# Which ring of SBUF buffers holds the early products of the first layer: four buffers of `stg` in place of two of `p`

## The chip, the cores and the metric

The kernel runs on one core of one Trainium2 chip. The metric is the device time of one execution in microseconds (us); lower is better. The kernel before was timed three times.

## The reference, cut to what matters

```python
# 1. a recurrence over 768 tokens, for 4 batches and 8 heads of width 48
for t in range(S):
    cur = np.einsum('bhd,bhe->bhde', u[None] * kt, vt)
    y[:, :, t] = np.einsum('bhd,bhde->bhe', rt, state + cur)
    state = w[None, :, :, None] * state + np.einsum('bhd,bhe->bhde', kt, vt)
# 2. x: the 3072 tokens of y, 384 wide
a = x @ w1            # 384 x 1024
b = x @ w2            # 384 x 1024
x2 = (a * b @ w3) @ w_out
# 3. second layer
h = x2 @ w_in         # 384 x 2048
out = (h * np.cos(h)) @ w_out2
```

The weights come as 64-bit floats and are decoded on the chip.

## The kernel before, in words

**Stages.** The recurrence is computed in 12 chunks of 64 tokens (`att_scores`, `att_mask`, `att_y`, `att_x`, `att_state`; `prep_*` scale the inputs). Tiles carry the chunk's number: `sc3_1` are the scores of chunk 3, half 1; `y3_1` and `st3_1` its output and state sums; `xp3_0` its transposes (L569). `att_x` copies these to `xh` (L574) and `xl` (L575), the high and low parts of the activations that the first layer multiplies. Two chunks fill one of six blocks `j` of 512 tokens.

**First layer.** For each block `j` and each of eight column tiles `m`, `ab(j, m)` computes two sums `a` and `b` in PSUM, each by three times three matmuls (high times high, high times low, low times high: L273, L274, L275). ScalarE then copies `a` to a buffer `p` in SBUF (L772), VectorE multiplies `b` into it (L773), and GpSimd issues a store of the product to DRAM, `pd` (L774). The copy and the product are issued with priority. `p0_4` is the product of `j` = 0, `m` = 4. The first two products of block 0 are computed in two halves of 256 tokens.

**Fold.** `w3 @ w_out` is multiplied once into `w34` (`fold_load`, `fold_mm`). Later the products are read back, multiplied by `w34` (`p3`), and the second layer follows (`stage_a` to `p4`).

**Rings of buffers.** `kt_(tag, ...)` gives the next of a fixed number of buffers: `p` has two, `stg` four. A buffer is given out again once its last reader is done; for a product that reader is its store. `stg` is used for a constant of the warm-up matmuls, later for half of the fold's decoded weights, for `x2` and for the output. PSUM has eight banks: three for `a` and `b`, two for the recurrence, three for sums.

**Order.** Each engine executes its instructions in the order of its queue. A scheduler fixes that order when the program is built, from its own estimate of when operands and buffers are ready. So a buffer that comes free earlier can move instructions. The program's order around the first layer is written out: `ORDER` lists the products, `SLOTS` says how many steps of the recurrence go ahead of each, `FOLD` how many of the fold. The fold's first step stands ahead of entry 14.

**Loads.** SP issues all loads. The scores need `rd` and `kd`, whose single buffers are loaded again for the next chunk when the scores of this one are done (L367), and then scaled on VectorE (L486).

Of the kernel before, what the change touches and what calls it, by code (L numbers as in the profile page):

```python
# [184 lines left out]
def kernel(  # L185
# [19 lines left out]
    with ExitStack() as own:  # L205
        held = own.enter_context(tc.tile_pool(name="held", bufs=1))
        dram = own.enter_context(tc.tile_pool(name="slow", bufs=1, space=DRAM))
        flag = held.tile([1, 1], I32, name="flag")
        chunked(
            tc, flag, rd_in, kd_in, rt_in, kt_in, vt_in, wT_in, u_in, w1_in, w2_in, w3T_in, wo_in, wi2_in, wo2_in, out  # L210
        )
        odd = nc.values_load(flag[0:1, 0:1], min_val=0, max_val=48)
        with tc.If(odd > 0):
            xc = dram.tile([out.shape[0], 384, 512], F32, name="xc")
            sequential(tc, rt_in, kt_in, vt_in, w_in, u_in, xc)
            plain(tc, xc, w1_in, w2_in, w3T_in, wo_in, wi2_in, wo2_in, out)
# [3 lines left out]
def chunked(  # L220
# [41 lines left out]
    def kt_(tag, shape, nm, dt=F32):  # L262
        return keep.tile(list(shape), dt, tag=tag, name=nm, bufs=BUFS[tag])

    def bank(nm, tag):
        return psum.tile([128, 512], F32, tag=tag, name=nm, bufs={"ab": 3, "att": 2, "acc": 3}[tag])
# [5 lines left out]
    def mm3(o, wh, wl, xh, xl, first, last):  # L272
        nc.tensor.matmul(o, wh, xh, start=first, stop=False)  # L273
        nc.tensor.matmul(o, wh, xl, start=False, stop=False)  # L274
        nc.tensor.matmul(o, wl, xh, start=False, stop=last)  # L275
# [7 lines left out]
    def flush():  # L283
        while late:
            late.pop(0)()
# [311 lines left out]
    halves, whole = [slice(0, 256), slice(256, 512)], slice(0, 512)  # L597
# [41 lines left out]
    def w12(m, n):  # L639
        g, i = divmod(m, 4)  # L640
        fs = slice(i * 128, (i + n) * 128)
        for which, hi, lo in ((1, w1h, w1l), (2, w2h, w2l)):
            if g not in hi:
                hi[g] = wp.tile([128, 3, 512], F32R, tag=f"g{g}", bufs=4, name=f"w{which}h{g}")
                lo[g] = wp.tile([128, 3, 512], F32R, tag=f"g{g}", bufs=4, name=f"w{which}l{g}")
            decode(w12_id[which, m], (hi[g][:, :, fs], lo[g][:, :, fs]))
# [6 lines left out]
    for ps in range(3):  # L653
        n = 128 * min(3, NM1 - 3 * ps)
# [42 lines left out]
    def fold_step(n):  # L697
        for _ in range(n):
            if folds:
                it = folds.pop(0)  # L700
                fold_load(*it)
                fold_pend.append(it)
            if len(fold_pend) > (2 if folds else 0):
                if not folds:
                    flush()
                fold_mm(*fold_pend.pop(0))
# [48 lines left out]
                nc.scalar.copy(s, acc[j][e])  # L755
                nc.sync.dma_start(out=x2d[j][:, e, :], in_=s)

    def ab(j, m, cols=slice(0, 512)):
        g, i = divmod(m, 4)
        fs = slice(i * 128, (i + 1) * 128)  # L760
        n = cols.stop - cols.start
        a = bank(f"a{j}_{m}", "ab")[:, 0:n]
        b = bank(f"b{j}_{m}", "ab")[:, 0:n]
        for t, wh, wl in ((a, w1h, w1l), (b, w2h, w2l)):
            for kk in range(3):
                mm3(
                    t, wh[g][:, kk, fs], wl[g][:, kk, fs], xh[j][:, kk, cols], xl[j][:, kk, cols], kk == 0, kk == 2
                )
        p = kt_("p", (128, 512), f"p{j}_{m}")[:, 0:n]

        with tc.high_priority(offset=-80):
            nc.scalar.copy(p, a)  # L772
            nc.vector.tensor_tensor(out=p, in0=p, in1=b, op=ALU.mult)  # L773
        nc.gpsimd.dma_start(out=pd[j][m][:, cols], in_=p)  # L774
# [43 lines left out]
    decays()  # L818
    flush()
    ab(0, 0, halves[0])  # L820
    prep_u(1)
    prep_g(1)
# [7 lines left out]
    att_state(1, 0)  # L830
    flush()
    ab(0, 1, halves[0])
    att_x(1, 1)
    att_state(1, 1)
# [11 lines left out]
    def advance(n):  # L846
        for _ in range(n):
            att_slot(*next(slots, (NSTEP, 0)))

    for i, (j, m) in enumerate(ORDER):  # L850
        advance(SLOTS[i])
        if i in (1, 6):
            w12({1: 4, 6: 6}[i], 2)
        fold_step(FOLD[i])
        flush()
        ab(j, m, halves[1] if j == 0 and m < 2 else whole)
    while folds or fold_pend:
        fold_step(1)
    att_cm.__exit__(None, None, None)
# [16 lines left out]
    for i in range(NBLK * NM1):  # L876
        j, m = divmod(i, NM1)
# [64 lines left out]
    for it in items + [None] * 5:  # L942
        if it:
            j, m = it
# [80 lines left out]
```

## Time and profile before

| what | value |
|---|---|
| time, median of 3 runs | 863.75 us (861.83 to 864.93) |
| the profiled execution | 865.14 us, of which 863.4 us from the first to the last instruction (the span) |
| mean granted TensorE clock | 0.99 of full speed |
| busy share of the span | PE 97%, VectorE (DVE) 64%, ScalarE (ACT) 48%, GpSimd (POOL) 4% |
| stores of products | 46 whole ones of 256 KB, median 2.8 us to landing |

PE is TensorE. In the profile, a bracket behind an instruction gives the time that its engine stood idle ahead of it and what ended that. The chain is the sequence of work that ended last, followed back from the end.

### The profile page before, as it was taken

To read this page: it belongs to the slowest core of one execution; us is meant where nothing else is said; L and a number is where in the kernel's file an instruction comes from. 1 tells how busy PE (TensorE), PEld (TensorE's weight loads), DVE (VectorE), ACT (ScalarE), POOL (GpSimd) and SP (SyncE) were. 2 spreads that over 40 slices of the span, in tenths; PEclk is the share of its full clock that TensorE was granted. 3 is DMA by queue.
4 is the path that set the end of the run, shared out by engine and by line. 5 is a ranking of instruction groups with operands and counts; after the bars stand their busy time and mean duration, and the time that the engine had idled before them with its cause. 6 is when DMAs were issued, how large, how long until landed. Compare 5 with 4: busy or idle time off the path is not lost.

```text
span 863.4 us, 14166 instructions
## 1 busy us (share of the span) xinstructions
PE 840.5 (97%) x5630; PEld 682.9 (79%) x5634; DVE 554.8 (64%) x839; ACT 415.6 (48%) x708; POOL 35.9 (4%) x66
## 2 busy tenths in 40 slices
PE   6987999999999999999999999999999999999997
PEld 3775778888888888888888888888888888888885
DVE  8876977786555534498956655655655655655552
ACT  4764555544553531255446445445545544544442
POOL 3000010010100001000000000000000000000000
PEclk9988999999999999999999999999999999999998
DMA  8757566565343263288952002001001100100101
GB/s 254 208 182 221 163 199 210 177 206 151 113 149 110 71 209 132 90 305 296 326 177 74 1 1 73 1 1 59 15 1 38 36 0 15 59 0 1 38 1 40
DMA packets 41161, 95.04 MB, mean 110 GB/s; under 512 B 4736, under 2 KB 6400, under 8 KB 41088
## 3 DMA queue, kind: packets, MB, share of 16 engines
q1 hardware_dynamic: 37072, 81.28, 30.0%
q0 software_dynamic: 3872, 12.59, 3.9%
q8 instruction: 46, 0.75, 0.4%
q10 hardware_dynamic: 144, 0.20, 0.1%
q14 instruction: 27, 0.22, 0.1%
HBM read 72.03 MB, written 22.02 MB: 109 GB/s over the span
## 4 chain that ended last, share of the span: by engine, by line
PE 94%; DVE 2%; DMA 1%; ACT 1%; issue 1%; ACTq 0%; DVEq 0%
PE p L274 12%; PE p L273 12%; PE p L275 12%; PE h L275 8%; PE h L273 8%; PE h L274 8%; PE a L273 4%; PE b L273 4%; PE b L275 4%; PE b L274 4%; PE a L274 4%; PE a L275 4%; PE y L554 3%; PE sc L518 2%; PE hps L409 2%; PE st L591 2%
## 5 line engine op out<-in xcount | busy, mean ns | idle before, releaser
L921 ACT ACTIVATE u<-h,qbias 128x512 f32<-128x512 f32 x96 | 66.2, 689 | 138.0 <-PE h L275 138.0
L922 DVE TENSOR_SCALAR n<-u 128x512 f32<-128x512 f32 x96 | 41.1, 428 | 138.0 <-ACT u L921 138.0
L275 PE MATMUL h<-x2h,wil 128*128 128x512 f32 x288 | 113.2, 393 | 0.0
L273 PE MATMUL h<-x2h,wih 128*128 128x512 f32 x288 | 113.1, 393 | 0.0
L274 PE MATMUL p<-gl,woh 128*128 128x512 f32 x288 | 113.1, 393 | 0.0
L274 PE MATMUL h<-x2l,wih 128*128 128x512 f32 x288 | 113.0, 392 | 0.0
L275 PE MATMUL p<-gh,wol 128*128 128x512 f32 x288 | 113.0, 392 | 0.0
L273 PE MATMUL p<-gh,woh 128*128 128x512 f32 x288 | 113.0, 392 | 0.0
L924 ACT ACTIVATE u<-n 128x512 f32<-128x512 f32 x96 | 60.9, 634 | 65.1 <-DVE n L923 65.1
L930 DVE TENSOR_TENSOR u<-u,h 128x512 f32<-128x512 f32 x96 | 66.0, 687 | 16.7 <-ACT u L924 16.7
L773 DVE TENSOR_TENSOR p<-p,b 128x512 f32<-128x512 f32 (+1 forms) x50 | 33.1, 661 | 62.4 <-PE b L275 35.7
L923 DVE SCALAR_TENSOR_TENSOR n<-n,u 128x512 f32<-128x512 f32 x96 | 66.4, 692 | 3.3
L936 DVE TENSOR_TENSOR gl<-u,gh 128x512 fp32r<-128x512 f32 x96 | 65.7, 685 | 0.7 <-ACT gh L932 0.7
L274 PEld LDWEIGHTS p<-gl,woh 128*128 128x128 f32 x288 | 54.1, 188 | 12.4
L275 PEld LDWEIGHTS h<-x2h,wil 128*128 128x128 f32 x288 | 54.1, 188 | 12.3
L273 PEld LDWEIGHTS h<-x2h,wih 128*128 128x128 f32 x288 | 54.1, 188 | 12.3
L274 PEld LDWEIGHTS h<-x2l,wih 128*128 128x128 f32 x288 | 54.1, 188 | 12.2
L273 PEld LDWEIGHTS p<-gh,woh 128*128 128x128 f32 x288 | 54.1, 188 | 12.2
L275 PEld LDWEIGHTS p<-gh,wol 128*128 128x128 f32 x288 | 54.1, 188 | 12.2
L772 ACT COPY p<-a 128x512 f32<-128x512 f32 (+1 forms) x50 | 28.3, 568 | 67.3 <-PE a L275 56.0
L273 PE MATMUL a<-xh,w1h 128*128 128x512 f32 (+1 forms) x150 | 60.4, 403 | 0.0
L932 ACT CAST gh<-u 128x512 fp32r<-128x512 f32 x96 | 58.9, 613 | 0.8 <-DVE u L930 0.8
(163 smaller groups left out, 1717.5 us busy)
## 6 DMA issues: line engine op xcount, KB each, us to landing
pr<-pd SPq DMA_DIRECT2D x48, 256.0 KB, 4.1
pd<-p POOLq DMA_DIRECT2D x46, 256.0 KB, 2.8
raw<-in_wo_dram SPq DMA_DIRECT2D x12, 768.0 KB, 5.0
raw<-in_w3T_dram SPq DMA_DIRECT2D x8, 768.0 KB, 5.0
raw<-in_wi_dram SPq DMA_DIRECT2D x8, 768.0 KB, 5.6
raw<-in_w_dram SPq DMA_DIRECT2D x6, 768.0 KB, 5.7
x2d<-x SPq DMA_DIRECT2D x18, 256.0 KB, 5.5
x2s<-x2d SPq DMA_DIRECT2D x18, 256.0 KB, 3.3
```

The source lines that it names most:

```text
L273: nc.tensor.matmul(o, wh, xh, start=first, stop=False)
L274: nc.tensor.matmul(o, wh, xl, start=False, stop=False)
L275: nc.tensor.matmul(o, wl, xh, start=False, stop=last)
L772: nc.scalar.copy(p, a)
L773: nc.vector.tensor_tensor(out=p, in0=p, in1=b, op=ALU.mult)
L921: head[0] = nc.scalar.activation(out=u, in_=h, func=AF.Identity, scale=INV_2PI, bias=qbias).ins
L922: nc.vector.tensor_scalar_add(out=n, in0=u, scalar1=RND)
L923: nc.vector.scalar_tensor_tensor(out=n, in0=n, scalar=RND, in1=u, op0=ALU.subtract, op1=ALU.subtract)
L924: nc.scalar.activation(out=u, in_=n, func=AF.Sin, scale=-TWO_PI)
L930: nc.vector.tensor_tensor(out=u, in0=u, in1=h, op=ALU.mult)
L932: nc.scalar.copy(gh, u)
L936: nc.vector.tensor_tensor(out=gl, in0=u, in1=gh.bitcast(F32), op=ALU.subtract)
```

## The change

A new argument of `ab`, `early`, true unless it is given, takes the product's buffer from the ring `stg` instead of `p`. The loop over `ORDER` gives it as true for entries 0 to 12. The two half products that are computed ahead of the loop are early as well. The remaining 35 entries keep the ring `p`. No instruction is added or removed.

```diff
-    def ab(j, m, cols=slice(0, 512)):
+    def ab(j, m, cols=slice(0, 512), early=True):
...
-        p = kt_("p", (128, 512), f"p{j}_{m}")[:, 0:n]
+        p = kt_("stg" if early else "p", (128, 512), f"p{j}_{m}")[:, 0:n]
...
-        ab(j, m, halves[1] if j == 0 and m < 2 else whole)
+        ab(j, m, halves[1] if j == 0 and m < 2 else whole, early=i < 13)
```

The built programs of before and after differ in the order of the queues and in what some instructions wait for. A number at the end of a name only tells buffers apart; in square brackets stand the semaphores that an instruction waits for, and `DMASW` is that of a store of GpSimd (the stores take `DMASW0` to `DMASW7` in turn).

ScalarE, at the second half of chunk 3's masks (`xa`, `xb`: operands of `y3_0`; `yt3_0`: the copy of `y3_0`):

```order
 L501 COPY zb_137<-kt_130 64x768 [waits Activation_49]
-L539 COPY xa_131<-am_133 64x512 [waits DVE_49,Activation_49]
-L540 COPY xb_132<-am_133 64x512 [waits Activation_49]
-L539 COPY xa_131<-am_133 64x512 [waits DVE_49,Activation_49]
-L540 COPY xb_132<-am_133 64x512 [waits Activation_49]
-L772 COPY p0_4_1076<-a0_4_1056 128x512 [waits DMASW4_49,PE_49]
+L772 COPY p0_4_1076<-a0_4_1056 128x512 [waits DMASW2_49,PE_49]
+L539 COPY xa_131<-am_133 64x512 [waits DVE_49,Activation_49]
+L540 COPY xb_132<-am_133 64x512 [waits Activation_49]
+L539 COPY xa_131<-am_133 64x512 [waits DVE_49,Activation_49]
+L540 COPY xb_132<-am_133 64x512 [waits Activation_49]
 L556 COPY yt3_0_1033<-y3_0_1016 128x384 [waits PE_49,Activation_49]
```

The copy of `a0_4` moves ahead of the masks' copies, and it waits for the third store (a half product) where it waited for the fifth (`p0_2`).

PE, from the last matmuls of `a0_1`'s second half to `y2_0`; before:

```order
L274 MATMUL a0_1_835<-xl0_381,w1h0_361 128x256
L275 MATMUL a0_1_835<-xh0_380,w1l0_362 128x256
L554 MATMUL y2_0_775<-va_134,xa_131 64x48 [waits DMAHW5_49,Activation_49]
L554 MATMUL y2_0_775<-vb_135,xb_132 64x48 [waits DMAHW6_49,Activation_49]
L554 MATMUL y2_0_775<-va_134,xa_131 64x48
```

and after:

```order
L275 MATMUL a0_1_835<-xh0_380,w1l0_362 128x256
L273 MATMUL b0_1_836<-xh0_380,w2h0_370 128x256 [waits Activation_49]
L274 MATMUL b0_1_836<-xl0_381,w2h0_370 128x256
L275 MATMUL b0_1_836<-xh0_380,w2l0_371 128x256
L273 MATMUL b0_1_836<-xh0_380,w2h0_370 128x256
```

The nine matmuls of `b0_1`, which stood behind `y2_0` and `st2_0`, now stand ahead of them. Likewise the last three of `b0_4` and the first six of `a0_5` move ahead of `y3_0`.

PE, between `b0_5` and the next block's products; before:

```order
L274 MATMUL b0_5_1142<-xl0_381,w2h1_824 128x512
L275 MATMUL b0_5_1142<-xh0_380,w2l1_825 128x512
L273 MATMUL a1_0_1181<-xh1_878,w1h0_361 128x512 [waits Activation_49]
L274 MATMUL a1_0_1181<-xl1_879,w1h0_361 128x512 [waits DVE_49]
L275 MATMUL a1_0_1181<-xh1_878,w1l0_362 128x512
```

and after:

```order
L275 MATMUL b0_5_1142<-xh0_380,w2l1_825 128x512
L273 MATMUL a1_0_1181<-xh1_878,w1h0_361 128x512 [waits Activation_49]
L518 MATMUL sc4_0_1229<-rd_127,kd_128 64x64 [waits DMAHW1_49,DMAHW3_49,DVE_49,PE_49]
L521 MATMUL sc4_0_1229<-rd_127,kd_128 64x64 [waits DMAHW4_49,DMAHW2_49]
L518 MATMUL sc4_0_1229<-rd_127,kd_128 64x64
```

The scores of chunk 4 stood behind `a1_0`, `b1_0`, `a1_1` and `b1_1`; now they come after the first matmul of `a1_0`, ahead of the other 35. On VectorE the order changes accordingly, and most of the fold's decoding moves behind later products. GpSimd's order is the same.

## Rows read from the trace of the kernel before

**Rows 1.** The page: busy time of each engine, share of the span, instructions.
```profile
PE 840.5 (97%) x5630; PEld 682.9 (79%) x5634; DVE 554.8 (64%) x839; ACT 415.6 (48%) x708; POOL 35.9 (4%) x66
```

**Rows 2.** Windows by stage: stretch, length, busy of PE, PEld, DVE, ACT, POOL, PEclk, DMA, GB/s.
```profile
40.00:80.00 40.00, 34.81 (x459) 28.56 (x457) 33.63 (x45) 21.55 (x37) 2.70 (x5) 0.91 0.69 203
80.00:120.00 40.00, 36.43 (x317) 29.63 (x318) 32.13 (x41) 18.72 (x32) 4.13 (x7) 0.91 0.59 185
120.00:160.00 40.00, 40.00 (x509) 32.40 (x508) 30.29 (x41) 25.04 (x42) 2.70 (x5) 1.00 0.67 201
```

**Rows 3.** PE's timeline, 50 to 172 us: start, duration, instruction, idle before.
```profile
50.97 0.45 PE L554 MATMUL y<-va,xa 128*64 128x48 f32 x2 [2.84 <-DMA rd<-in_rd_dram]
54.77 0.58 PE L273 MATMUL b<-xh,w2h 128*128 128x256 f32 x1
56.64 0.41 PE L275 MATMUL b<-xh,w2l 128*128 128x256 f32 x1
83.57 0.34 PE L554 MATMUL y<-va,xa 128*64 128x48 f32 x1 [5.34 <-ACT yt L556]
171.71 0.42 PE L273 MATMUL fa<-fwh,w3h 128*128 128x384 f32 x1
```

**Rows 4.** The chain, 73 to 87 us: start, duration, what.
```profile
73.99 8.48 DMA pd<-p
83.03 0.49 ACT yt L556
83.57 1.95 PE y L554 x32
85.52 0.83 PE xp L569 x3
86.35 0.43 PE a L273
```

**Rows 5.** ScalarE's timeline, 76 to 83 us.
```profile
76.36 0.62 ACT L540 COPY xb<-am 64x512 f32<-64x512 f32 x1
82.55 0.58 ACT L772 COPY p<-a 128x512 f32<-128x512 f32 x1 [5.57 <-DMA pd<-p]
```

**Rows 6.** Waits of the whole span: who waited for whom, total, times, longest.
```profile
ACT p L772 <- DMA pd<-p: 11.1, 3, 5.6
```

**Rows 7.** Stores of products, from issue to landing: minimum, median, maximum.
```profile
DMA to landing us min/median/max: 2.3/2.9/8.5
```

**Rows 8.** Windows of one microsecond, columns as in Rows 2.
```profile
50.00:51.00 1.00, 0.03 (x1) 0.03 (x1) 1.00 (x3) 0.67 (x2) 0.00 (x0) 0.55 1.01 209
81.00:82.00 1.00, 0.00 (x0) 0.00 (x0) 0.00 (x0) 0.00 (x0) 0.00 (x0) 0.50 0.99 397
```

**Rows 9.** The chain, 121 to 126 us, at the full clock.
```profile
121.92 1.07 PE y L554 x32
122.99 0.48 PE xp L569 x3
123.47 0.24 PE a L273
124.88 0.85 PE st L591 x32
```

**Rows 10.** VectorE's timeline, 60 to 150 us; the last row is the product `p1_7`.
```profile
60.13 0.56 DVE L575 TENSOR_TENSOR xl<-xp,xh 128x384 fp32r<-128x384 f32 x1 [2.46 <-ACT xh L574]
79.66 1.23 DVE L486 TENSOR_TENSOR rd<-rd,t 128x1024 f32<-128x1024 f32 x1 [1.68 <-DMA rd<-in_rd_dram]
87.38 0.95 DVE L332 TENSOR_TENSOR w1l<-dt,w1h 128x768 fp32r<-128x768 f32 x1
88.24 1.22 DVE L486 TENSOR_TENSOR kd<-kd,t 128x1024 f32<-128x1024 f32 x1
149.72 0.69 DVE L773 TENSOR_TENSOR p<-p,b 128x512 f32<-128x512 f32 x1 [1.63 <-ACT p L772]
```

**Rows 11.** A window from `rd`'s scaling to `p1_2`'s product, columns as in Rows 2.
```profile
79.66:107.44 27.78, 23.87 (x208) 19.44 (x209) 21.02 (x27) 14.22 (x23) 2.17 (x4) 0.88 0.57 179
```

## The prediction

> **What bounds the kernel now.** I read the page's busy times first: TensorE (PE) is busy 97% of the span, the others far less [rows 1]. So time can come only from PE's idle time and from stretches at a lowered clock. The windows by stage say where these are: of 40 us PE works 34.81 in 40 to 80 us and 36.43 in 80 to 120 us, at a mean granted clock of 0.91; from 120 us on it works 40.00 of 40 at 1.00 [rows 2]. Behind 120 us PE is the bound without a gap, so whatever makes it reach that point earlier should last to the end; the other engines must then keep up in a schedule that is shifted earlier.
>
> PE's timeline shows two large gaps: 2.84 us ahead of 50.97 and 5.34 us ahead of 83.57 [rows 3]. The chain of waits explains the second. The store of `p0_2` is issued at 73.99 and lands 8.48 us later, at 82.47; then come `yt` at 83.03, the copy of `y3_0`, and `y3_1` on PE at 83.57 [rows 4]. ScalarE's timeline has the link between them: it is through with the masks' copies at 76.36 + 0.62 = 76.98, and the next thing in its queue is the copy of `a0_4` into a `p` buffer, which waits 5.57 us for that store [rows 5]. The copy of `y3_0` only stands behind it. Over the whole span such waits of the copy come to 11.1 us in three, but only this one stands in the chain [rows 4, 6].
>
> The gap costs more than its length. In the 1-us windows the clock is granted at 0.50, the level of 1.2 GHz, at 81 us, after PE has stood since 78.23 (83.57 − 5.34); it is 0.55 at 50 us, behind the other gap [rows 3, 8]. At that level `y3_1` takes 1.95 us, its transposes 0.83 and each row of `a0_5` 0.43 [rows 4]; the same work at the full clock takes 1.07, 0.48 and 0.24 [rows 9].
>
> **The change, part by part.** Nothing is added or removed, so the sum has only waits, order and clock.
>
> *The wait of `p0_4`.* From the four buffers, its copy waits for the third store, a half product's, where it waited for the fifth. It also stands ahead of the masks' copies now. The third store belongs to the second half of `p0_0`, whose matmuls precede those of `b0_1` at 54.77 [rows 3]; even at the longest landing, 8.5 us [rows 7], it is down before 73.99. The copy's 0.58 us then lies under the 8.48 us in which ScalarE had slack, while PE has the last three matmuls of `b0_4` and six of `a0_5` to do. Behind 76.98 ScalarE goes straight to `yt`, 0.49 [rows 4], so `y3_1` can start at 77.5 in place of 83.57: 6.1 us. Seven matmuls of `a0_5` that followed then are done ahead of it: 7 × 0.24 = 1.7 [rows 9]. Together **7.8**. It is more than the 5.34 of the gap, because it assumes that the matmuls which moved ahead find room; what bounds that comes under "the first gap".
>
> *The clock behind the gap.* PE does not stand, so the clock has no reason here to fall: (1.95 − 1.07) + (0.83 − 0.48) + 3 × (0.43 − 0.24) = **1.8** [rows 4, 9].
>
> *The first gap.* `b0_1`'s nine matmuls move out of 54.77 to 57.05 (56.64 + 0.41) into the wait ahead of 50.97; what they took behind it, 2.28 us at the lowered clock, is gone [rows 3]. In their place five matmuls of `a0_2` come into that slow stretch, 5 × (0.43 − 0.24) = 0.95 longer than they would be later. That leaves some 1.3 us of room for nine more matmuls ahead of `y3_0`, 9 × 0.24 = 2.2: if the clock stays down here, `y3_0` starts up to 0.9 us late, which takes 0.9 from the 7.8. If the clock stays up, since PE stands less, the lost half comes back, and the masks may come earlier too: VectorE stands 2.46 us at 60 us for the transposes that PE brings [rows 10]. I bound this term by −0.9 and +2.5 and take **+0.5**: the clock was still lowered after 2.84 us of standing, and `b0_1` at full clock fills less than half of that.
>
> *The scores of chunk 4, moved forward.* `sc4_0` now stands ahead of 35 matmuls, and PE's queue waits there for `kd`'s scaling on VectorE. PE is there about 77.5 + 1.07 + 0.48 + 0.85 + 12 × 0.24 = 82.8 (`y3_1`, transposes, state sums, the rest of `a0_5`, `b0_5` and one of `a1_0`) [rows 9]. `rd`'s scaling waited for its load until 79.66 [rows 10], and that load needs only the scores of chunk 3, which hardly move. Behind it stand `w1l` (0.95), `xl` (0.56), the first step of a decode (about as `xl`) and `kd` (1.22): by these rows 79.66 + 1.23 + 0.95 + 0.56 + 0.56 + 1.22 = 84.2; starts overlap by some 0.1 each, so about 83.7. PE waits some **−0.8**, with bounds of 0 (the decode elsewhere, PE later) and −1.4.
>
> *What must keep up.* If PE is some 9 us earlier at 107 us, VectorE must be nearly so. From `rd`'s scaling at 79.66, a load's time that does not move, to the product of `p1_2` at 107.44 it works 21.02 of 27.78 us [rows 11]: it can gain 6.8, and the other 2.5 must come from the time between a product and the next use of its PSUM bank, and from the decode that moves behind. I take nothing here, and price it as a rival. The fold's decoding is pushed back on VectorE: its second half now precedes `p1_7`'s product (149.72) and is needed by matmuls at 171.71 [rows 3, 10]; 22 us, less the shift of 9, hide it.
>
> Sum: 7.8 + 1.8 + 0.5 − 0.8 = **9.3 us**. The profiled execution took 865.14, so 855.8; it lay 1.4 above the median of the runs, so **854.4 us** against 863.75.
>
> **The rivals.**
> - *The masks become the bound.* If the scores' masks and the products on VectorE come late between 85 and 120 us, part of the gap opens again there. For it speaks that VectorE's room is 6.8 and the shift 9.3 [rows 11]; against it, that much of its work in the stretch (the decode) is moved behind. Gain 5 to 8: about **857.3**.
> - *The wait is not what it seems.* If another thing held ScalarE, say a store that is quick and a semaphore that comes late for another reason, the masks' copies and `yt` would only trade places: **863.7**. Against it stands the DMA share of 0.99 in the wait with nothing busy [rows 8]. The Trainium skill, "DMA: Bandwidth & Descriptors", section "Anatomy of one DMA — SWDGE (gpsimd) path", gives some 2.0 us plus the bytes at 436 GB/s for such a store; an estimate by it for 256 KB is 2.6 us, the store would land at 76.6, ahead of the masks' end, and the change would win nothing. The median of the stores, 2.9, is close to that, the 8.48 of this one is not [rows 4, 7], and the trace decides.
> - *Slower: PE waits at `sc4_0`.* The 35 matmuls that covered the loads and scalings of `rd` and `kd` now stand behind the wait. Were `kd` scaled as late as before, at 88.24 + 1.22 = 89.46 [rows 10], PE would stand 6.7 us, not 0.8, and lose perhaps 1.5 to a lowered clock: gain 2, **861.9**. It turns into a loss when the scaling ends later than some 91.5. For that the loads would have to land 8 us later than now, in competition with the stores that are issued earlier; the store that took 8.48 shows that this is possible at this DMA share. At 96 us: **868**.
>
> **How the numbers follow.** Forecast 0.70, its own range 852 to 856.5 (the bounds of the first gap and of `sc4_0`: sum 7.3 to 12.1, the upper end hardly reached in full); masks 0.15; no effect 0.07; the third rival 0.08, of which 0.06 for a loss and 0.02 for the small gain. A measurement of this kernel can tell about 0.3%, 2.6 us, from no change: faster 0.85 (the first two), within 0.09, slower 0.06. To leave out no more than 2 in 10, the range runs from 851.5 to 859.0.
>
> **What the profile of after would show.** ScalarE's wait of 5.57 for `pd` and PE's gap ahead of `y3_1` gone; the clock near 1.00 from 75 to 90 us; PE busy some 39 of 40 in 80 to 120 us; the waits of the copy for stores from 11.1 to 1 or less. A PE gap ahead of `sc4_0` names the third rival, gaps of PE behind masks or products in 90 to 120 the first. I am wrong if a gap of more than 2 us opens anywhere behind 75 us, or if stores issued earlier slow the loads of chunks 3 and 4.

## The result, and the profile after

The changed kernel took 855.42 us (median of six runs, 853.77 to 856.81), the kernel before 863.54 us in the six runs timed with it. The ratio is 0.9906 with a 95% interval of 0.989 to 0.9921, that is 6.8 to 9.5 us less; the forecast was 854.4. The profiled execution has a span of 853.5 us and a mean granted clock of 1.00.

The windows by stage, columns as in [rows 2]:

```profile
40.00:80.00 40.00, 38.17 (x545) 31.47 (x544) 38.25 (x51) 27.06 (x47) 3.25 (x6) 1.00 0.76 237
80.00:120.00 40.00, 39.93 (x361) 31.10 (x359) 27.96 (x36) 19.71 (x32) 3.78 (x7) 1.00 0.57 179
120.00:160.00 40.00, 40.00 (x484) 32.68 (x483) 33.97 (x44) 24.34 (x41) 3.25 (x6) 1.00 0.65 193
```

PE stands 1.83 us in 40 to 80 us where it stood 5.19, and 0.07 in 80 to 120 us where it stood 3.57. The clock is at its higher level in all three. All that is left of the gaps, but for 0.09 us, is in PE's timeline at 48 to 52 us:

```profile
48.91 0.38 PE L273 MATMUL b<-xh,w2h 128*128 128x256 f32 x1 [0.88 <-ACT p L772]
50.75 0.32 PE L554 MATMUL y<-va,xa 128*64 128x48 f32 x2 [0.53 <-ACT xa L539]
51.39 0.26 PE L554 MATMUL y<-vb,xb 112*64 112x48 f32 x1 [0.33 <-ACT xb L540]
75.19 0.26 PE L554 MATMUL y<-va,xa 128*64 128x48 f32 x1
```

The nine matmuls of `b0_1` now stand in the first gap, which had 2.84 us of standing. The last row is `y3_1`: it starts at 75.19 with no bracket, where it started at 83.57 behind 5.34 us [rows 3]. ScalarE's timeline shows why:

```profile
69.97 0.58 ACT L772 COPY p<-a 128x512 f32<-128x512 f32 x1
...
73.64 0.62 ACT L540 COPY xb<-am 64x512 f32<-64x512 f32 x1
74.47 0.48 ACT L556 COPY yt<-y 128x384 f32<-128x384 f32 x1 [0.22 <-PE y L554]
```

`p0_4`'s copy runs at 69.97 and waits for nothing, and the copy of `y3_0` follows the masks' copies, as it does not in [rows 5]. The answer on waits has no row of this copy for a store any more; before it had 11.1 us in three [rows 6]. The stores themselves still take 2.3, 3.1 and 8.1 us (minimum, median, maximum) to landing, hardly other than in [rows 7]: what has changed is that no copy waits for them.

**One measure for all runs.** A whole span holds two things that change from run to run: how early the first chunks end (the copy of `y1_0` starts at 34.65 to 36.78 us in the profiles here) and how long the end takes (7.7 to 9.1 us from the start of the last copies to the end of the span). So I compare starts on ScalarE: stretch A from the copy of `y1_0` to that of `y2_1` (first gap), B from there to the copy of `y4_0` (second gap), C from there to the last copies of the output. The expectations call the copy of `y1_0` "the first copy of y" and give A + B + C. Its ends in the profile of the change and, below, of the kernel before:

```profile
35.78 0.47 ACT L556 COPY yt<-y 128x384 f32<-128x384 f32 x1
...
845.65 1.98 ACT L908 COPY o<-p 128x512 f32<-128x512 f32 x3 [5.06 <-PE p L275]
```

```profile
35.86 0.47 ACT L556 COPY yt<-y 128x384 f32<-128x384 f32 x1
...
855.73 1.98 ACT L908 COPY o<-p 128x512 f32<-128x512 f32 x3 [5.06 <-PE p L275]
```

The table is worked out from such rows of every profile. "Clock" is the mean granted clock in the window 48 to 58 us, "stood" PE's standing at 47 to 53 us.

| kernel | A | B | C | A+B+C | stood | clock |
|---|---|---|---|---|---|---|
| before | 23.37 | 53.48 | 743.02 | 819.87 | 3.0 | 0.66 |
| before, again (e7) | 22.37 | 55.16 | 743.02 | 820.55 | 3.0 | 0.83 |
| change | 21.00 | 45.83 | 743.04 | 809.87 | 1.7 | 1.00 |
| change, again (e8) | 22.86 | 46.24 | 743.04 | 812.14 | 2.0 | 0.83 |
| change, third (e10) | 21.11 | 46.42 | 743.04 | 810.57 | 1.9 | 1.00 |
| halves only (e1) | 21.00 | 46.20 | 743.18 | 810.38 | 1.7 | 1.00 |
| wholes only (e2) | 22.60 | 46.85 | 743.05 | 812.50 | 3.3 | 0.83 |
| wholes, filled late (e3) | 23.56 | 45.08 | 743.04 | 811.68 | 2.3 | 1.00 |
| store held (e4) | 21.15 | 49.45 | 743.16 | 813.76 | 1.9 | 1.00 |
| wholes, filled (e5) | 21.12 | 47.44 | 743.04 | 811.60 | 1.2 | 1.00 |
| three deep (e6) | 21.01 | 46.92 | 743.13 | 811.06 | 1.7 | 1.00 |
| change, filled (e9) | 21.53 | 45.80 | 743.04 | 810.37 | 0.8 | 1.00 |
| decode later (e11) | 19.09 | 48.56 | 743.67 | 811.32 | 0.5 | 1.00 |

C is the same to 0.02 us in all five profiles of the kernel before and the change: what is won before 113 us lasts to the end, and nothing is lost behind.

### The profile page after: what moved, and what is told of

The parts are those of the page before. It is cut to its first block, busy times and chain, and to the rows that moved or that the text cites. A ratio compares the mean times of both kernels' runs of the same rounds, so it can differ in the third digit from the quotient of the medians.

```text
span 853.5 us, 14160 instructions
## 1 busy us (share of the span) xinstructions
PE 836.5 (98%) x5630; PEld 679.0 (80%) x5634; DVE 554.3 (65%) x839; ACT 415.2 (49%) x708; POOL 35.1 (4%) x66
## 4 chain that ended last, share of the span: by engine, by line
PE 96%; DVE 2%; ACT 1%; DMA 1%; issue 0%; ACTq 0%; DVEq 0%
PE p L274 12%; PE p L275 12%; PE p L273 12%; PE h L275 8%; PE h L273 8%; PE h L274 8%; PE a L273 4%; PE a L274 4%; PE a L275 4%; PE b L273 4%; PE b L275 4%; PE b L274 4%; PE y L554 3%; PE sc L518 2%; PE hps L409 2%; PE st L591 2%
## 5 line engine op out<-in xcount | busy, mean ns | idle before, releaser
L273 PE MATMUL b<-xh,w2h 128*128 128x512 f32 (+1 forms) x150 | 58.3, 389 | 1.0 <-ACT p L772 0.9
```

## The experiments

**e1: only the half products in the other ring.** My theory: the first reuse of a buffer counts. Rival: the whole products need four buffers too.

```diff
-        ab(j, m, halves[1] if j == 0 and m < 2 else whole, early=i < 13)
+        ab(j, m, halves[1] if j == 0 and m < 2 else whole, early=i < 2)
```

> Only the four half products (blocks of 256 tokens) take their buffer from stg; all whole products keep the two buffers of p. PE's order up to the fold is that of the change but for a few rows. My theory is that what counts is the first reuse of a buffer, not how many products lie in the four-buffer ring: with the halves out of p, the copies of p0_2 and p0_3 find free buffers, p0_2's product and store come early (store issued near 61 us in place of 74), and p0_4's copy no longer waits. So the whole gain is there: span 853 to 855 us, PE's gap ahead of y3_1 gone, clock 1.00 from 48 to 90 us. The rival, that four buffers are needed for the whole products too, gives a wait of p0_4's copy for p0_2's store again and a span of 858 to 862.

Measured: 856.97 us, ratio 0.9924 (0.9897 to 0.9952), span 854.4. Against the first profile of the change, A is the same and B 0.4 longer. GpSimd issues `p0_2`'s store at 60.83 in place of 73.99 [rows 4] (third row here):

```profile
54.74 0.54 POOL L774 DMA_DIRECT2D pd<-p  x1 [1.78 <-DVE p L773]
59.20 0.54 POOL L774 DMA_DIRECT2D pd<-p  x1 [3.92 <-DVE p L773]
60.83 0.54 POOL L774 DMA_DIRECT2D pd<-p  x1 [1.08 <-DVE p L773]
```

and `p0_4`'s copy does not wait, though the whole products still share two buffers. One later copy waits 5.34 us for a store, at 94 us; PE loses 0.15 us in 92 to 120 us. So in the profile four of the fifteen moves bring nearly all of it (by the runs the two are not told apart: the intervals overlap). With the halves out of `p`, `p0_2` finds a free buffer, and its product goes ahead of the decoding and scaling on VectorE.

**e2: only the whole products in the other ring.**

```diff
-        ab(j, m, halves[1] if j == 0 and m < 2 else whole, early=i < 13)
+        ab(j, m, halves[1] if j == 0 and m < 2 else whole, early=2 <= i < 13)
-    ab(0, 0, halves[0])
+    ab(0, 0, halves[0], early=False)
```

and the same for `ab(0, 1, halves[0])`.

> The reverse: the half products stay in p, the whole products of entries 2 to 12 take stg. PE's order up to the masks of chunk 3 is then that of the kernel before. The first gap (ahead of 50.97 us, 2.84 us) and its lowered clock should stay as before, and the second gap (5.34 us ahead of y3_1) and its lowered clock should go. By the terms 5.34 + 1.83 that is 7.2 us: span 855.5 to 857. If the early order of b0_1 was what also cured the second gap, the span is 860 or more; if the first gap costs nothing at the end, it is 853.5 as for the whole change.

Measured: 858.88 us, ratio 0.9938 (0.9916 to 0.996), span 857.5, A + B + C 7.4 us shorter than in the first profile before. The first gap stays (2.92 us) and its clock falls; the second gap is gone:

```profile
51.92 0.26 PE L554 MATMUL y<-va,xa 128*64 128x48 f32 x1 [2.92 <-DMA rd<-in_rd_dram]
52.57 0.26 PE L554 MATMUL y<-vb,xb 112*64 112x48 f32 x1 [0.33 <-ACT xb L540]
74.46 0.50 PE L273 MATMUL b<-xh,w2h 128*128 128x512 f32 x1 [0.68 <-ACT p L772]
```

The two gaps are separate: `b0_1`'s early order is not what cures the second one. The span is 0.5 us over the range given for it; this execution's `y1_0` came 0.9 us later than that of before.

**e3 and e5: the first gap filled with matmuls without use.** Is the first gap's price the clock, or that no useful matmul stands in it? Both fill the gap of e2 and leave its order alone. In e3 the matmuls write `y2_0`'s bank:

```diff
-        y = bank(f"y{c}_{g}", "att")
+        y = bank(f"y{c}_{g}", "att"); [nc.tensor.matmul(y[0:D, 0:384], flat(zb)[0:112, 0:D], flat(zb)[0:112, 0:384], start=True, stop=True) for _ in range(4 * ((c, g) == (2, 0)))]
```

> As the run with the whole products only, and four matmuls without use (48 x 384) ahead of y2_0, in the first gap, their result overwritten by y2_0. They take PE 2 to 2.6 us of the 2.84 it stands and move nothing else forward. If the term of the first gap is the clock (it stays at 1.00 from 50 to 57 us), the span is 2 to 3 us shorter than without them: 853 to 854.5. If what counted there was b0_1's nine matmuls being done in the gap, the filling brings nothing or costs up to 0.5 us: 855.5 to 857.5.

Measured: 857.03 us, ratio 0.9909 (0.9888 to 0.9931), span 856.0. The span lies in the range of the rival, but the run does not test it: that bank was still being read by the masks, so the filling waited 2.27 us and came behind the gap. It lengthened A by 1.0, yet the clock stayed up, and B is 1.8 shorter. In e5 they have a bank of their own:

```diff
+    z = bank("fill", "acc"); [nc.tensor.matmul(z[0:D, 0:384], flat(zb)[0:112, 0:D], flat(zb)[0:112, 0:384], start=True, stop=True) for _ in range(3)]
```

> The whole products only in stg, as before, and three matmuls without use (48 x 384, from the state operand zb, into a PSUM bank that nothing else uses) ahead of y2_0. They can start some 0.7 us after PE stops and keep it busy 1.9 to 2.4 of the 2.9 us of the first gap; no useful matmul moves forward. If the term of the first gap is the clock, it stays at 1.00 from 50 to 60 us and, from the first copy of y to the last copy of the output, the kernel takes 1.5 to 2.5 us less than without them (812.5 there): 810 to 811, span 853.5 to 856. If b0_1's matmuls done in the gap are what counts, it stays at 812 to 813.

Measured: 857.6 us, ratio 0.9923 (0.9897 to 0.9948), span 856.7, 0.7 over its range. PE's timeline:

```profile
49.51 2.14 PE L844 MATMUL fill<-zb 112*48 112x384 f32 x6 [0.86 <-ACT zb L501]
52.24 0.26 PE L554 MATMUL y<-vb,xb 112*64 112x48 f32 x1 [0.33 <-ACT xb L540]
72.64 0.50 PE L273 MATMUL b<-xh,w2h 128*128 128x512 f32 x1 [0.68 <-ACT p L772]
80.26 0.20 PE L591 MATMUL st<-va,za 128*48 128x48 f32 x1 [0.38 <-issue]
```

The clock stays at 1.00 and A is 1.5 us shorter than in e2 (21.12 against 22.60), though not one useful matmul moved. All of the difference lies behind the copy of `y2_0`, where the clock was low in e2: from that copy to that of `y2_1` it is 4.69 us in e2 and 3.20 here. That is the clock's share there. Over the whole, 0.9 of it remains (811.60, between the two forecasts), since B is 0.6 longer; 0.4 of this is a standing of PE that the profile gives no cause for (last row).

**e4: the store held back.** The buffers of e1, with `p0_2`'s store kept until chunk 3's first mask is written. GpSimd adds a mask value to one element of the product, so that this kernel no longer computes the reference, and the store stands behind that:

```diff
+        nc.gpsimd.tensor_tensor(out=q[0:1, 0:1], in0=q[0:1, 0:1], in1=am[0:1, 0, 0, 0:1], op=ALU.add)
+        nc.gpsimd.dma_start(out=o, in_=q)
```

emitted ahead of `p0_4`'s matmuls.

> As the run with the half products only, but the store of p0_2 is held on GpSimd until the first mask of chunk 3 is written (one element of p0_2 gets a mask value added so that the store has to wait). Buffers are as there; only the store is late again, at 72 to 73 us, with a landing of 6 to 8.5 us at 78 to 81. The scheduler now puts p0_4's copy behind the copy of y3_0 on ScalarE. By my theory the wait is back (ScalarE idle some 4 to 6 us ahead of p0_4's copy for a store), but y3_1 no longer stands behind it: PE waits only at b0_5's bank, 2 to 4 us, with some clock: span 856 to 859. If the late store was not the cause, ScalarE does not wait and the span is as with the half products alone.

Measured: 860.55 us, ratio 0.9958 (0.9939 to 0.9977), span 857.6. The chain of waits, 70 to 82 us:

```profile
70.74 0.57 DVE p L779
71.32 0.28 issue
71.60 7.17 DMA pd<-p
78.78 0.02 issue
78.80 0.02 ACT p L778
...
79.28 0.48 ACT va L593
79.76 0.01 issue
79.77 0.48 ACT vb L593
80.26 0.04 issue
80.30 0.90 PE xp L569 x3
```

The waits stand in the timelines of ScalarE and of PE:

```profile
78.80 0.58 ACT L778 COPY p<-a 128x512 f32<-128x512 f32 x1 [3.51 <-DMA pd<-p]
```

```profile
80.30 0.90 PE L569 MATMUL xp<-ident,yt 128*128 128x128 f32 x3 [3.20 <-ACT vb L593]
```

The wait is back, in two details otherwise than thought. `p0_4` has the buffer of `p0_3`, not that of `p0_2`, so the store in the chain is `p0_3`'s, which nothing held back: issued at 71.60, it landed 7.17 us later. And PE waits 3.20 us ahead of `xp3_0` and not at `b0_5`'s bank: the copies `va` and `vb` of the state sums, which end its wait, stand behind the copy of `a0_4` in ScalarE's queue. The clock falls too: 0.90 in 75 to 92 us, and the transposes take 0.90 us instead of 0.48 [rows 9]. B is 3.3 us longer than in e1; by the runs alone the two are not told apart, since the intervals overlap. The copy of `y3_0` now stands ahead of the waiting copy, and the wait costs B 3.3 us where it cost about 8 in the kernel before; no run moved that copy alone. So what counts is when the store of the buffer's last product is issued and what stands behind the copy that waits for it.

**e6: three buffers for all products.**

```diff
-    BUFS = {"wx": 4, "wf": 4, "p": 2, "ph": 3, "pl": 3, "stg": 4, "raw": 2, "dt": 1}
+    BUFS = {"wx": 4, "wf": 4, "p": 3, "ph": 3, "pl": 3, "stg": 3, "raw": 2, "dt": 1}
```

> All products in the ring p, which gets three buffers; stg gets three in place of four. If only the depth at the first reuse counts, p0_4's buffer is then that of the second half of p0_1, whose store is long down, and the order around both gaps is that of the change: span 853 to 855.5, no wait of the copy for a store over 1 us before 90 us. If four free buffers are needed, or if the smaller stg makes the fold or the output wait, the span is 856 or more.

Measured: 857.16 us, ratio 0.9917 (0.9892 to 0.9943), span 856.3. No copy waits for a store, and A and the copies of `y3_0` and `y3_1` come as in the change (38.70 and 41.00 us behind that of `y1_0`; 38.69 and 41.00 there). The rest of B is 1.1 longer, of which 0.93 is again a standing without a cause in the profile:

```profile
79.59 0.20 PE L591 MATMUL st<-vb,zb 112*48 112x48 f32 x1 [0.93 <-issue]
```

One buffer more in one ring removes the same waits as the second ring. The span is 0.8 us over the forecast; besides those 1.1 us, its end is 1.3 us longer than in the profile of the change.

**e7, e8 and e10: the same two kernels again.** Unchanged, for further profiles.

> The kernel before once more, for a second profile. The first one lay 1.4 us above the median. If that was the moment at which the clock fell in its first gap or the start, this profile shows it elsewhere: a span of 861 to 864.5, both gaps there within 0.2 us (2.8 and 5.3), and the loss by the lowered clock different by 0.5 to 1.5 us. If both profiles agree within 0.3 us from the first copy of y to the last of the output (819.9), the distance to the median has another cause.

> The changed kernel once more, for a second profile: span 853 to 855.5, and from the first copy of y to the last of the output within 0.3 us of the first one's 809.9, since it has no stretch at a lowered clock that could differ. If it differs by 1 us or more, the spread of the runs does not come from the clock.

> The changed kernel a third time, timed beside the run with the filling, for a third profile: either 809.9 or 812.1 from the first copy of y to the last of the output, within 0.4, by whether the clock falls behind the first gap; median 855 to 856.5.

Measured: before 867.37 us with a span of 865.7 (the forecast was 861 to 864.5); the change 856.37 and a median of 856.57 (ratio 0.9907, 0.989 to 0.9924), spans 854.7 and 856.3. In e8 the clock fell behind the first gap, in e10 it did not, and A + B + C is 812.14 and 810.57, where 809.9 was forecast for e8 and 809.9 or 812.1 for e10, within 0.4. As written for e8, a difference of 1 us or more would have spoken against the clock; but that took for granted that the clock does not fall in this kernel, and here it did. One microsecond of e8's windows (columns as in [rows 8]):

```profile
52.00:53.00 1.00, 1.00 (x31) 1.00 (x30) 1.00 (x2) 1.00 (x3) 0.54 (x1) 0.50 0.33 47
```

So one and the same program has two lengths of A, 21.0 or 21.1 and 22.9. Of the 1.9 us between the first profile and e8, 1.5 lie behind the copy of `y2_0`, where the clock is low (4.81 us to the copy of `y2_1` against 3.32); 0.4 lie ahead of it and are not the clock's. In the kernel before the clock falls in both profiles, for a shorter time in e7 (0.83 against 0.66 in the window); but the second gap of e7 is longer, 6.00 us.

**e9: the change, with its first gap filled.** The line of e5 with two matmuls, in the changed kernel.

> The changed kernel, and two matmuls without use (48 x 384, from zb, into a PSUM bank of their own) behind a0_1, in what is left of the first gap; they cut PE's standing there from 1.7 to about 1.0 us and make y2_0 up to 0.2 us later. By the clock theory the changed kernel loses some 2 us in those executions in which the clock falls there (812.1 from the first copy of y to the last of the output) and none in the others (809.9); with the filling it does not fall: 809.8 to 810.6 here, median 0.5 to 1.5 us below that of the changed kernel timed beside it. If the spread has another cause, the median is the same or 0.2 us longer.

Measured: 855.29 us, ratio 0.9895 (0.9878 to 0.9913), span 853.9; its runs lie within 0.8 us, those of the change beside it within 3.8. The clock is 1.00, and A + B + C 810.37, as forecast. But the clock does not explain that spread: the slowest run of the change beside it, 858.02 us, is the profiled e10, in which the clock did not fall. Its span is 2.4 us longer than that of e9, and only 0.2 of this is in A + B + C; it starts 1.0 later and its end is 1.2 longer. The intervals of e9 and e10 overlap too, so the gain of 1.3 us over the change is not shown.

**e11: the decoding written later.**

```diff
-    w12(2, 2)
     prep_d(2)
...
     prep_g(2)
+    w12(2, 2)
```

> The changed kernel with the decoding of the weights of columns 2 and 3 written behind the scalings of chunk 2 instead of ahead of them. VectorE is busy without a break ahead of the masks that end the first gap; with some 2 us of decoding moved behind, the masks come up to 2 us earlier and PE's 1.7 us of standing at 48 to 51 us shrink to under 1. But a0_2 needs those weights: if their decoding is then late, PE waits ahead of a0_2 instead, 0.5 to 2 us. Forecast 0.5 to 1.5 us faster than the change; the rival is the same or up to 1 us slower.

Measured: 855.8 us, ratio 0.99 (0.9882 to 0.9917), span 855.6. A is 1.9 us shorter than in the change, as forecast. It is given back in B, through the decoding, though later than the rival said:

```profile
70.56 0.50 PE L273 MATMUL b<-xh,w2h 128*128 128x512 f32 x1 [2.38 <-ACT w2h L330]
```

No variant here is shown to beat the change.

## Why the prediction was right, point by point

- **The wait of `p0_4` and its clock** were 7.8 + 1.8 = 9.6 us. They fall into B: 53.48 and 55.16 before (mean 54.3), 45.83, 46.24 and 46.42 after (mean 46.2), so 8.2; e2, which leaves the first gap's order, gives 7.37 and 8.05 over A + B + C (812.50 against the two profiles before). The mechanism is right: e1 agrees that it is the buffer's first reuse, and in e4 the wait returns with a store issued late. The term of 7.8 is too large by some 1.4. In the first profile, B before less the gap's 5.34 and the clock's 1.8 is 46.3, and B after is 45.83, with PE standing next to nothing. So there was hardly more to win than the standing and the clock, but the term counted 2.5 us of moved matmuls besides. It also took 8.48 us for ScalarE's slack; that is the store's time, of which ScalarE stood 5.57 [rows 5].
- **The first gap**, taken as +0.5 between −0.9 and +2.5, is A: 23.37 and 22.37 before; 21.00, 22.86 and 21.11 after. Single pairs give −0.5 to 2.4, the means 1.2. The range turned on the right question, whether the clock stays up; I had not seen that the same program does both. By e5 against e2, a fall of the clock there costs 1.5 us of A.
- **The wait at `sc4_0`**, put at −0.8, did not come: this is the step that failed. I had written that the load of `rd` "needs only the scores of chunk 3, which hardly move". They moved by nearly 3 us: SP's timeline, before and after, has the load of `rd`:

```profile
71.94 0.79 SPq L367 DMA_DIRECT2D rd<-in_rd_dram  x2
```

```profile
69.13 0.79 SPq L367 DMA_DIRECT2D rd<-in_rd_dram  x2
```

  and VectorE's and PE's timelines after:

```profile
75.19 1.23 DVE L486 TENSOR_TENSOR rd<-rd,t 128x1024 f32<-128x1024 f32 x1
...
78.61 1.22 DVE L486 TENSOR_TENSOR kd<-kd,t 128x1024 f32<-128x1024 f32 x1
79.75 0.95 DVE L478 TENSOR_TENSOR rt<-rt,kt 128x768 f32<-128x768 f32 x1
```

```profile
80.98 0.27 PE L518 MATMUL sc<-rd,kd 48*64 48x64 f32 x1
```

  The load is issued 2.8 us earlier, and its two parts land within 5.1 to 5.5 us where they took 6.4 to 7.2 before. So `rd` is scaled at 75.19, with no wait, in place of 79.66 [rows 10]. `kd` is done at 79.83, and PE comes to `sc4_0` at 80.98, with no wait. So the third rival, a long wait there, did not occur.
- **The sum** of 9.3 us is what the profiles give by their means (820.2 − 810.9 = 9.3), and that is in part luck: 1.4 too much for the wait of `p0_4`, against 0.8 for a wait that did not come and 0.7 too little for the first gap.
- **What must keep up** did: C is equal to 0.02 us, and PE works without a gap from 92 us on:

```profile
92.00:120.00 28.00, 28.00 (x264) 22.22 (x262) 17.62 (x23) 12.93 (x22) 2.70 (x5) 1.00 0.55 173
```

  The first rival did not occur, and the fold's later decoding cost nothing.
- **The change without effect**: refuted by the 6.8 to 9.5 us that were won and by the row at 69.97. By the Trainium skill, "DMA: Bandwidth & Descriptors", section "Anatomy of one DMA — SWDGE (gpsimd) path", an estimate for such a store was 2.6 us. The traces agree for most of them (minimum 2.3, median 2.9 [rows 7]), not for those that were waited for: 8.48 us [rows 4], and 7.17 in e4. Why these take so long no run here tells apart; the DMA engines were busy 0.99 in the wait [rows 8].
- **From the profile to the median.** By the medians the change is worth 8.1 us. I took 1.4 us off the forecast because the profile of before lay that far above its median. That did not carry over: the change's first profiled execution lay 0.1 below its median, e8 1.0 above that median, e10 1.5 above its own. That is most of why 854.4 was 1.0 low. The runs of the kernel before show what goes with its high profiles: of the 30 for which a mean clock is given, nine at 0.996 or 0.997 take 862.8 us in the mean, fourteen at 0.991 to 0.993 take 864.3, and five at 0.989 or 0.990 take 865.9. Both profiled executions are among the five. Why the clock fell further in these is open.

One word of the description is to be mended: the copy and the product of `ab` have an offset of −80, which ranks them 80 places later for the scheduler, not earlier.

## What to carry to other kernels

When a copy into a ring of buffers waits for a store, ask when that store was issued and what stands behind the copy in its queue: here a product whose store was issued 13 us later than with the change (73.99 against 61.33) held up, through one copy, matmuls that had nothing to do with it. A deeper ring helps where the first reuse meets the late store; four moves, or one buffer more, did about as much as fifteen moves (ratios 0.9924 and 0.9917 against 0.9906, with intervals that overlap). And before an order is changed, every load whose buffer is freed by moved work is to be moved along in the estimate.

## What was not expected

- The clock's fall behind a short standing of PE differs between executions of the same program. With 1.7 to 2.0 us of standing at 47 to 53 us it fell in one of six profiles, with 2.3 us (e3) it did not, with 3.0 to 3.3 us it fell in three of three. Where the same order of work was seen with and without the fall, the fall cost 1.5 us (e8 against the change, e2 against e5).
- PE stood 0.22 to 0.93 us at the state sums of chunk 3 in four profiles (e5, e6, e8, e10), and the profile names nothing that it waited for; in the first profile of the change it did not. What it was stays open.
